# A fixed order for the first attention of a fused attention and two-MLP kernel, and other units kept on chip

## The chip, the cores and the metric
One core of a Trainium2 chip runs the kernel, in one launch. The metric is the device time of that launch in microseconds (us). The kernel before took 708.74 us (median of three runs, 707.78 to 709.10).

## The reference
Three layers follow each other, all in fp32:

```
attention, B=2, H=8, S=576, D=64:
  scores = q k^T / sqrt(D) + min(-(cum_i - cum_j), 0), causal   # cum: running sum of max(s, 0)
  attn   = softmax(scores);  x = attn v                         # 1152 tokens x 512
layer 1:  h = x w_in (512 x 2048);  g = h if h > 0 else exp(h) - 1;  x = g w_out
layer 2, four experts e, p = domain_probs normalised:
  out += p[:, e] * (max(x w1[e], 0) w2[e])                      # 512 x 1024 each
```

`moe_w_in` and `moe_w_out` come as 64-bit words; a part of the kernel turns them into fp32 ("decodes" them).

## The kernel before, in words
**Groups.** The 1152 tokens are worked on in three groups, of 256, 448 and 448 (`GROUPS`). Group 0 goes through attention, layer 1 and layer 2; then layer 1 runs for groups 1 and 2, and layer 2 for both together. The attention of group 1 is cut into some seventy parts that a `Background` object strews between the products of layers 1 and 2 of group 0; that of group 2 is strewn into layer 1 of group 1.

**Layer 1.** `w_in` and `w_out` are cut into 16 units (`NAB`) of 128 hidden columns. `layer1` (line 701) runs slots k = 0 to 17: slot k issues up-projection k (`up1`, line 729, called u0, u1, ...), then its activation (exp on line 733, relu on line 736, the combination `gt` on line 737), and down-projection k - 2 (`down1`, line 716), which adds into four banks `acc0` to `acc3`. A bank `up` is free again when line 737 has read it, and there are two.

**Decoding.** For group 0 a unit comes as two halves of 512 KB, 32 in the order (0,0), (1,0), (0,1), (2,0), ... `fetch_halves` (line 126) issues their loads on SP's queue into places borrowed from tiles that are not yet in use (`places`: `gt`, `wu`, `wr`, `cd`, `yh`, ...); the first 25 have a place of their own, the last 7 wait until an earlier half in the same place has been decoded. `decode_halves` (line 139) turns one half into fp32: on ScalarE (ACT) an Abs (line 158) and a copy to `z` (line 165; for the first four halves on VectorE, line 161), on VectorE (DVE) two words (lines 166 and 168). The ACT instructions are pinned behind everything traced before on ACT. A unit that is not kept on chip is also written to DRAM (`w_dec`, line 171, on POOL's queue) for the later groups; units 12 to 15 stay in `wr`. `DEC` says after which step of the first attention how many halves are decoded; `advance` (line 637) decodes on, two or three per slot, ahead of layer 1, and orders the loads (`fetch`) and splits (`prepare`, line 102: a copy on ACT and `split_lo`, line 87, on DVE) of the weights that follow.

**The first attention** (`attention_first`, line 265) does group 0: 256 tokens, eight heads in four pairs hp. Per pair: `scores` (products of q and k and of the bias parts `cump` and `cumm`, lines 313 to 323, a bank per head; heads 6 and 7 use the banks of heads 2 and 3 again), `probabilities` (DVE line 333, then an exponential on ACT, line 335), `normalise` (DVE), `transposes` (PE line 352, copied out by ACT on line 353) and `values` (PE line 361, copied by ACT on line 363). `cum_parts` writes the running sum and its parts to DRAM for the later groups, `cum_columns` (line 223) turns a piece of it into columns, `probabilities_of` (line 251) normalises the layer-2 weights. `keep_warm` (line 365) issues products of the identity that nobody reads.

**What sets the order.** A planner orders each engine's instructions, by program order and by when its own model takes them to be ready; `issue_after` queues a block behind an instruction on the same engine, and `keep_in_program_order` pins one. Tiles of a pool that closes give their bytes to the next one: a tile there waits for the users of the earlier tiles on its bytes. The pool `first` holds the tiles of the first attention and the places `cd`; when slot 14 begins its background part (`First`, line 762), it closes and the pool `att` takes its bytes, for the attention of groups 1 and 2. The first loads of that attention (lines 429 and 430 into `pt`) are queued behind the last coded half on SP.

Of the kernel before, what the change touches and what calls it, by code (L numbers as in the profile page):

```python
# [45 lines left out]
DEC = [1, 2, 3, 4]  # L46
# [4 lines left out]
N_WR, N_WU, N_GT, N_CD = 2, 1, 3, 5  # L51
# [3 lines left out]
def tile_kernel(ctx, tc, qT, kT, v, s, w64, w, probs, out):  # L55
# [39 lines left out]
    def fetch(n):  # L95
        if n >= NU and (n - NU) % NAB in kept:
            fetched[n] = kept[(n - NU) % NAB]
            return
        fetched[n] = t = sb([128, 1024], "raw", 3)
        SP.dma_start(out=t, in_=w[n - NAB] if n < NU else w_dec[(n - NU) % NAB])  # L100

    def prepare(n):
# [9 lines left out]
    small = [("yh", 1, 1), ("yl", 1, 1)] + [("raw", 3, 1)] * 3 + [("xa", 1, 3), ("ox", 1, 3)]  # L112
    turn = ([("gt", 3, 1)] * N_GT + [("wu", 5, 2)] * N_WU + [("wr", N_WR, 2)] * N_WR
            + [("cd", N_CD, 1)] * N_CD + small * 2)
# [9 lines left out]
    n_coded, n_decoded, last_coded = [0], [0], [None]  # L124
# [13 lines left out]

    def decode_halves(upto):

        while n_decoded[0] < min(upto, len(order)):
            i = n_decoded[0]
            n, part = order[i]
            if part == 0:
                if n % 2 == 0:
                    if n < NAB - N_KEPT:
                        pair = sb([128, 2, 1024], "wu", 5)  # L150
                    else:
                        pair = sb([128, 2, 1024], "wr", N_WR)
                        kept[n], kept[n + 1] = pair[:, 0], pair[:, 1]
                    units[n], units[n + 1] = pair[:, 0], pair[:, 1]
            x, m = coded.pop(i), units[n][:, 512 * part:512 * part + 512]
            high, low, mi = x[:, :, 1], x[:, :, 0], m.bitcast(I32)
            tc.keep_in_program_order(
                ACT.activation(m, high.bitcast(F32), AF.Abs, scale=2.0 ** -112))  # L158
            z = sb([128, 512], f"z{i % 2}", 1, I32)
            if i < N_LOW:  # L160
                tc.keep_in_program_order(DVE.tensor_scalar(
                    z, low.bitcast(U32), 7.49 / 2 ** 32, None, op0=ALU.mult))
            else:
                tc.keep_in_program_order(
                    ACT.activation(z, low.bitcast(U32), AF.Copy, scale=7.49 / 2 ** 32))  # L165
            DVE.scalar_tensor_tensor(out=mi, in0=mi, scalar=3, in1=z,
                                     op0=ALU.logical_shift_left, op1=ALU.bitwise_or)
            DVE.scalar_tensor_tensor(out=mi, in0=high, scalar=-2 ** 31, in1=mi,
                                     op0=ALU.bitwise_and, op1=ALU.bitwise_or)
            if part and n not in kept:  # L170
                POOL.dma_start(out=w_dec[n], in_=units[n])
            n_decoded[0] += 1
            fetch_halves()
# [3 lines left out]
    make_identity(nc, ident)  # L177

# [10 lines left out]

    zero = sb([64, 256], "zero", 1)  # L190
    POOL.memset(zero, 0.0)

# [69 lines left out]
    def attention_first(x):  # L265
# [31 lines left out]
        with tc.issue_after(high.ins), tc.issue_after(low.ins):  # L297
            cum_parts()
# [57 lines left out]
        def values(hp):  # L356
            o = ps(f"acc{(hp + 2) % 4}", 1)
            for c, q0 in ((0, 0), (1, 128)):
                for j in range(2):
                    h = 2 * hp + j  # L360
                    PE.matmul(o[64 * j:64 * j + 64, q0:n], vv[:, c, 64 * h:64 * h + 64],
                              ptt[:, h, 256 * c:256 + 128 * c], start=c == 0, stop=c == 1)
            ACT.activation(x[:, hp], o[:, :n], AF.Copy)
# [9 lines left out]
        with tc.issue_after(keep_warm(12).ins):  # L373
            first = scores(0)
            with tc.issue_after(first.ins), tc.issue_after(low.ins):
                cum_columns(0, 4)
                cum_columns(1, 4)
            scores(1)
            scores(2)
        probabilities(0)  # L380
        decode_halves(DEC[0])
        with tc.issue_after(scores(3).ins):
            keep_warm(6)
        probabilities(1)
        with tc.issue_after(normalise(0).ins):
            shares.extend((probabilities_of(0, n // 128), probabilities_of(T2, NCH)))
        with tc.issue_after(transposes(0).ins):
            keep_warm(4)
        probabilities(2)
        normalise(1)  # L390
        transposes(1)
        values(0)
        decode_halves(DEC[1])
        probabilities(3)
# [3 lines left out]
        decode_halves(DEC[2])  # L398
        normalise(3)
        transposes(3)  # L400
        values(2)
        values(3)
        decode_halves(DEC[3])
# [354 lines left out]
    attention_first(x_first)  # L758
    pr_first, pr_later = shares
    xs = [None, None, None]  # L760

    class First:
# [3 lines left out]
        def __call__(self, at):  # L766
            if at > BG_FROM[0]:
                if self.got is None:
                    first_stack.close()
# [13 lines left out]
    for c in range(NCC):  # L783
        ACT.activation(yh[:, c], yacc[c], AF.Copy)
        split_lo(yl[:, c], yacc[c], yh[:, c])
    pr = pr_first
# [316 lines left out]
```

## Time and profile before

| | us |
|---|---|
| median of three runs (lowest, highest) | 708.74 (707.78, 709.10) |
| the profiled execution, its own time | 710.54 |
| its span, first to last instruction | 708.4 |
| PE busy in the span | 696.6 (98%) |
| DVE busy | 561.7 (79%) |
| ACT busy | 382.4 (54%) |
| POOL busy | 15.6 (2%) |

All later numbers in us are counted from the start of the span. Timelines merge equal instructions that follow each other; their lengths overlap a little, so the spacing of two starts says more than a length. "Idle before" is the time that the engine stood still ahead of a row, with what it waited for. The clock of a window is the share of TensorE's full speed that the chip granted.

### The profile page before, as it was taken

To read this page: it belongs to the slowest core of one execution; us is meant where nothing else is said; L and a number is where in the kernel's file an instruction comes from. 1 tells how busy PE (TensorE), PEld (TensorE's weight loads), DVE (VectorE), ACT (ScalarE), POOL (GpSimd) and SP (SyncE) were. 2 spreads that over 40 slices of the span, in tenths; PEclk is the share of its full clock that TensorE was granted. 3 is DMA by queue.
4 is the path that set the end of the run, shared out by engine and by line. 5 is a ranking of instruction groups with operands and counts; after the bars stand their busy time and mean duration, and the time that the engine had idled before them with its cause. 6 is when DMAs were issued, how large, how long until landed. Compare 5 with 4: busy or idle time off the path is not lost.

```text
span 708.4 us, 10218 instructions
## 1 busy us (share of the span) xinstructions
PE 696.6 (98%) x3670; PEld 595.6 (84%) x3670; DVE 561.7 (79%) x1146; ACT 382.4 (54%) x773; POOL 15.6 (2%) x36
## 2 busy tenths in 40 slices
PE   8999999999999999999999999999999999999997
PEld 7888788887878887888899988888888888888886
DVE  7799788797868898876975469988888888788765
ACT  5799798786768788866644344322222223332320
POOL 5011000000000000000000000000000000000000
PEclk9899999999999999999999999999999999999999
DMA  8999855655554433113530000111111111111002
GB/s 299 409 368 373 271 174 154 193 166 157 174 185 140 141 125 102 41 47 128 210 140 0 1 1 0 60 60 60 60 61 59 60 60 59 61 60 59 1 0 105
DMA packets 34578, 85.45 MB, mean 121 GB/s; under 512 B 3440, under 2 KB 13888, under 8 KB 34528
## 3 DMA queue, kind: packets, MB, share of 16 engines
q1 hardware_dynamic: 32576, 78.23, 32.7%
q0 software_dynamic: 1952, 6.57, 2.3%
q8 instruction: 29, 0.48, 0.3%
q14 instruction: 21, 0.17, 0.1%
HBM read 75.88 MB, written 8.91 MB: 120 GB/s over the span
## 4 chain that ended last, share of the span: by engine, by line
PE 86%; ACT 7%; DVE 3%; issue 1%; DMA 1%; POOL 0%; SPq 0%; DVEq 0%; ACTq 0%; POOLq 0%
PE acc L626 38%; PE up L626 16%; PE att L938 11%; PE up L938 8%; PE att L581 3%; PE att L554 3%; ACT z L165 2%; ACT wu L158 2%; PE att L509 1%; PE att L502 1%; PE att L504 1%; DMA pt<-in_kT 1%; ACT e L736 1%; PE att L370 1%; PE acc L716 1%
## 5 line engine op out<-in xcount | busy, mean ns | idle before, releaser
L626 PE MATMUL acc<-w,h 128*128 128x512 f32 x672 | 172.0, 392 | 0.0
L626 PEld LDWEIGHTS acc<-w,h 128*128 128x128 f32 x672 | 126.1, 188 | 23.0 <-ACT h L948 0.2
L626 PE MATMUL acc<-gt,wu 128*128 128x448 f32 x384 | 87.8, 372 | 0.0
L948 ACT ACTIVATE h<-c 128x448 fp32r<-128x448 f32 x48 | 27.4, 573 | 111.7 <-DVE c L954 111.7
L683 DVE SCALAR_TENSOR_TENSOR ox<-acc,pr,ox 128x512 f32<-128x512 f32 x105 | 78.6, 748 | 11.1 <-PE acc L626 9.1
L87 DVE TENSOR_TENSOR wu<-raw,wu 128x1024 fp32r<-128x1024 f32 x56 | 68.4, 1223 | 19.5 <-ACT wu L106 17.3
L626 PEld LDWEIGHTS acc<-gt,wu 128*128 128x128 f32 x384 | 70.1, 188 | 7.8 <-issue 2.6
L106 ACT ACTIVATE wu<-raw 128x1024 fp32r<-128x1024 f32 x56 | 59.1, 1055 | 15.8 <-PE acc L626 14.1
L938 PE MATMUL att<-S,top 128*128 128x448 f32 x288 | 66.3, 365 | 0.0
L938 PEld LDWEIGHTS att<-S,top 128*128 128x128 f32 x288 | 54.0, 188 | 6.7 <-issue 0.2
L626 PE MATMUL acc<-wu,gt 128*128 128x512 f32 x192 | 56.8, 411 | 0.0
L626 PE MATMUL up<-yh,wu 128*128 128x256 f32 x256 | 52.5, 287 | 0.0
L949 DVE SCALAR_TENSOR_TENSOR h<-c,h 128x448 fp32r<-128x448 f32 x48 | 29.8, 623 | 18.7 <-ACT h L948 18.7
L938 PE MATMUL up<-x2a,top 128*128 128x448 f32 x192 | 44.2, 366 | 0.0
L626 PEld LDWEIGHTS up<-yh,wu 128*128 128x128 f32 x256 | 41.8, 190 | 2.6 <-issue 1.7
L626 PE MATMUL up<-xa,wu 128*128 128x448 f32 x192 | 43.5, 371 | 0.0
L626 PE MATMUL up<-ox,wu 128*128 128x448 f32 x192 | 41.5, 366 | 0.8 <-DVE e L741 0.8
L544 ACT ACTIVATE p<-p,nm 128x384 f32<-128x384 f32 (+4 forms) x56 | 34.5, 616 | 13.6 <-DVE nm L539 13.2
L948 ACT ACTIVATE h<-up 128x448 fp32r<-128x448 f32 x16 | 8.7, 545 | 59.5 <-PE up L938 59.5
L938 PEld LDWEIGHTS up<-x2a,top 128*128 128x128 f32 x192 | 35.9, 188 | 4.8 <-ACT p L963 0.6
L626 PEld LDWEIGHTS up<-ox,wu 128*128 128x128 f32 x192 | 36.0, 188 | 4.0 <-DVE e L741 1.1
L626 PEld LDWEIGHTS acc<-wu,gt 128*128 128x128 f32 x192 | 32.8, 189 | 6.9 <-issue 2.5
(215 smaller groups left out, 1245.6 us busy)
## 6 DMA issues: line engine op xcount, KB each, us to landing
raw<-in_w SPq DMA_DIRECT2D x38, 512.0 KB
raw<-in_w SPq DMA_DIRECT2D x16, 1024.0 KB
raw<-w_dec SPq DMA_DIRECT2D x24, 512.0 KB
w_dec<-wu POOLq DMA_DIRECT2D x12, 512.0 KB, 7.4
cd<-in_w SPq DMA_DIRECT2D x5, 512.0 KB
xa<-in_w SPq DMA_DIRECT2D x5, 512.0 KB
k<-in_kT SPq DMA_DIRECT2D x8, 288.0 KB
cbp<-cum_d SPq DMA_DIRECT2D x16, 144.0 KB
```

Of the source, the lines that this page charges most:

```text
L87: DVE.tensor_tensor(out=lo, in0=x, in1=hi.bitcast(F32), op=ALU.subtract)
L106: ACT.activation(t[:, 0], x, AF.Copy)
L158: ACT.activation(m, high.bitcast(F32), AF.Abs, scale=2.0 ** -112))
L165: ACT.activation(z, low.bitcast(U32), AF.Copy, scale=7.49 / 2 ** 32))
L544: ACT.activation(p, p, AF.Exp, bias=nm, scale=-1.0, accum_out=sm)
L554: PE.transpose(pt[:cb[c + 1] - cb[c], m, :], p[:, cb[c]:cb[c + 1]], ident)
L581: PE.matmul(o[64 * j:64 * j + 64, qs:nq], job["v"][:n, c, 64 * j:64 * j + 64], job["pt"][:n, j, c, qs:nq], start=c == 0, stop=c == n_c - 1)
L626: PE.matmul(o, a[m], b[n], start=first and i == 0, stop=last and i == 2)
L683: DVE.scalar_tensor_tensor(out=o_sb, in0=o, scalar=pr[:, i, e:e + 1], in1=o_sb, op0=ALU.mult, op1=ALU.add)
L938: PE.matmul(bank, tops[q][:, m, op, cs], x[:, n, c], start=first and c + i == 0, stop=c == 1 and i == 2, skip_group_check=True)
L948: ACT.activation(h[:, 0, u, cs], c, AF.Relu)
L949: DVE.scalar_tensor_tensor(out=h[:, 1, u, cs], in0=c, scalar=0.0, in1=h[:, 0, u, cs].bitcast(F32), op0=ALU.max, op1=ALU.subtract)
```

## The change
`attention_first` is traced in a region in which PE, ACT and DVE issue their instructions exactly as written. In it the order is new: scores 0 and 1, probabilities 0 and 1, scores 2 and 3, and then normalise, probabilities, transposes and values, staggered. The two later `keep_warm` blocks are gone and the first has 8 products for 12. The Abs of a half can be traced ahead of the rest of its decoding (`begin_half`). `cum_columns` and `probabilities_of` move to slot 14 of layer 1, on DVE behind the last decoded word. Units 0 to 3 are kept in `wr`, units 4 to 15 are written to DRAM. Coded halves use three `wu` tiles in place of one and two `wr`, and the last seven go into `cd`, `yh` and `yl` again, in place of `yh`, `yl`, `raw`, `xa`. `zero` is set before `mask`.

```diff
--- before.py
+++ after.py
@@ -43,12 +43,12 @@
 BG_FROM = [14, 0, 0]
 BG_TO = [1, 1, 0]
 
-DEC = [1, 2, 3, 4]
+DEC = [1, 2, 4]
 AHEAD = 10
 
 N_LOW = 4
 
-N_WR, N_WU, N_GT, N_CD = 2, 1, 3, 5
+N_WR, N_WU, N_GT, N_CD = 2, 3, 3, 5
 N_KEPT = 2 * N_WR
 
 @with_exitstack
@@ -97,7 +97,7 @@
             fetched[n] = kept[(n - NU) % NAB]
             return
         fetched[n] = t = sb([128, 1024], "raw", 3)
-        SP.dma_start(out=t, in_=w[n - NAB] if n < NU else w_dec[(n - NU) % NAB])
+        SP.dma_start(out=t, in_=w[n - NAB] if n < NU else w_dec[(n - NU) % NAB - N_KEPT])
 
     def prepare(n):
 
@@ -109,9 +109,9 @@
 
     order = [(0, 0)] + [h for n in range(NAB - 1) for h in ((n + 1, 0), (n, 1))] + [(NAB - 1, 1)]
 
-    small = [("yh", 1, 1), ("yl", 1, 1)] + [("raw", 3, 1)] * 3 + [("xa", 1, 3), ("ox", 1, 3)]
-    turn = ([("gt", 3, 1)] * N_GT + [("wu", 5, 2)] * N_WU + [("wr", N_WR, 2)] * N_WR
-            + [("cd", N_CD, 1)] * N_CD + small * 2)
+    twice = [("cd", N_CD, 1)] * N_CD + [("yh", 1, 1), ("yl", 1, 1)]
+    turn = ([("gt", 3, 1)] * N_GT + [("wu", 5, 2)] * N_WU + twice
+            + [("raw", 3, 1)] * 3 + [("xa", 1, 3), ("ox", 1, 3)] + twice + [("xa", 1, 3)])
     places = [(tag, bufs, n, i) for tag, bufs, n in turn for i in range(n)]
     coded, freed_by, last_in = {}, [], {}
     for i, (tag, bufs, many, k) in enumerate(places):
@@ -121,7 +121,7 @@
         else:
             freed_by.append(-1)
         last_in[tag][-1] = i
-    n_coded, n_decoded, last_coded = [0], [0], [None]
+    n_coded, n_decoded, last_coded, last_word = [0], [0], [None], [None]
 
     def fetch_halves(upto=len(order)):
 
@@ -136,6 +136,21 @@
                                          in_=w64[n, :, 1024 * part:1024 * part + 1024])
             n_coded[0] += 1
 
+    begun = {}
+
+    def begin_half(i):
+        n, part = order[i]
+        if part == 0 and n % 2 == 0:
+            if n >= N_KEPT:
+                pair = sb([128, 2, 1024], "wu", 5)
+            else:
+                pair = sb([128, 2, 1024], "wr", N_WR)
+                kept[n], kept[n + 1] = pair[:, 0], pair[:, 1]
+            units[n], units[n + 1] = pair[:, 0], pair[:, 1]
+        begun[i] = m = units[n][:, 512 * part:512 * part + 512]
+        tc.keep_in_program_order(
+            ACT.activation(m, coded[i][:, :, 1].bitcast(F32), AF.Abs, scale=2.0 ** -112))
+
     def decode_halves(upto):
 
 
@@ -144,18 +159,10 @@
         while n_decoded[0] < min(upto, len(order)):
             i = n_decoded[0]
             n, part = order[i]
-            if part == 0:
-                if n % 2 == 0:
-                    if n < NAB - N_KEPT:
-                        pair = sb([128, 2, 1024], "wu", 5)
-                    else:
-                        pair = sb([128, 2, 1024], "wr", N_WR)
-                        kept[n], kept[n + 1] = pair[:, 0], pair[:, 1]
-                    units[n], units[n + 1] = pair[:, 0], pair[:, 1]
-            x, m = coded.pop(i), units[n][:, 512 * part:512 * part + 512]
+            if i not in begun:
+                begin_half(i)
+            x, m = coded.pop(i), begun.pop(i)
             high, low, mi = x[:, :, 1], x[:, :, 0], m.bitcast(I32)
-            tc.keep_in_program_order(
-                ACT.activation(m, high.bitcast(F32), AF.Abs, scale=2.0 ** -112))
             z = sb([128, 512], f"z{i % 2}", 1, I32)
             if i < N_LOW:
                 tc.keep_in_program_order(DVE.tensor_scalar(
@@ -165,16 +172,19 @@
                     ACT.activation(z, low.bitcast(U32), AF.Copy, scale=7.49 / 2 ** 32))
             DVE.scalar_tensor_tensor(out=mi, in0=mi, scalar=3, in1=z,
                                      op0=ALU.logical_shift_left, op1=ALU.bitwise_or)
-            DVE.scalar_tensor_tensor(out=mi, in0=high, scalar=-2 ** 31, in1=mi,
-                                     op0=ALU.bitwise_and, op1=ALU.bitwise_or)
+            last_word[0] = DVE.scalar_tensor_tensor(out=mi, in0=high, scalar=-2 ** 31, in1=mi,
+                                                    op0=ALU.bitwise_and, op1=ALU.bitwise_or)
             if part and n not in kept:
-                POOL.dma_start(out=w_dec[n], in_=units[n])
+                POOL.dma_start(out=w_dec[n - N_KEPT], in_=units[n])
             n_decoded[0] += 1
             fetch_halves()
 
 
     ident = sb([128, 128], "ident", 1)
     make_identity(nc, ident)
+
+    zero = sb([64, 256], "zero", 1)
+    POOL.memset(zero, 0.0)
 
     mask = sb([128, S], "mask", 1)
     POOL.memset(mask, 0.0)
@@ -186,13 +196,6 @@
         m = maskp[64 * j:64 * j + 64]
         POOL.affine_select(out=m, in_=m, compare_op=ALU.is_ge, fill=-BIG, base=0,
                            pattern=[[-1, 64]], channel_multiplier=1)
-
-    zero = sb([64, 256], "zero", 1)
-    POOL.memset(zero, 0.0)
-
-
-
-
 
 
     cum = sb([B * H, S], "cum", 1)
@@ -294,8 +297,7 @@
             high = ACT.activation(t[:B * H], cum[:, 0:n], AF.Copy, scale=sign)
             low = DVE.scalar_tensor_tensor(out=t[64:], in0=cum[:, 0:n], scalar=sign,
                                      in1=t[:B * H].bitcast(F32), op0=ALU.mult, op1=ALU.subtract)
-        with tc.issue_after(high.ins), tc.issue_after(low.ins):
-            cum_parts()
+        cum_parts()
 
 
 
@@ -354,7 +356,7 @@
             return last
 
         def values(hp):
-            o = ps(f"acc{(hp + 2) % 4}", 1)
+            o = ps(f"acc{hp}", 1)
             for c, q0 in ((0, 0), (1, 128)):
                 for j in range(2):
                     h = 2 * hp + j
@@ -370,37 +372,32 @@
                 last = PE.matmul(o, ident, ident, start=True, stop=True)
             return last
 
-        with tc.issue_after(keep_warm(12).ins):
-            first = scores(0)
-            with tc.issue_after(first.ins), tc.issue_after(low.ins):
-                cum_columns(0, 4)
-                cum_columns(1, 4)
-            scores(1)
-            scores(2)
-        probabilities(0)
-        decode_halves(DEC[0])
-        with tc.issue_after(scores(3).ins):
-            keep_warm(6)
-        probabilities(1)
-        with tc.issue_after(normalise(0).ins):
-            shares.extend((probabilities_of(0, n // 128), probabilities_of(T2, NCH)))
-        with tc.issue_after(transposes(0).ins):
-            keep_warm(4)
+        keep_warm(8)
+        for hp in (0, 1):
+            scores(hp)
+        for hp in (0, 1):
+            probabilities(hp)
+        for hp in (2, 3):
+            scores(hp)
+        normalise(0)
         probabilities(2)
+        transposes(0)
         normalise(1)
+        probabilities(3)
         transposes(1)
+        begin_half(0)
         values(0)
-        decode_halves(DEC[1])
-        probabilities(3)
         normalise(2)
         transposes(2)
         values(1)
-        decode_halves(DEC[2])
+        begin_half(1)
         normalise(3)
+        decode_halves(DEC[0])
         transposes(3)
         values(2)
+        decode_halves(DEC[1])
         values(3)
-        decode_halves(DEC[3])
+        decode_halves(DEC[2])
 
 
     def attention_parts(g, x):
@@ -755,8 +752,9 @@
 
 
     x_first = sb([128, NCC, GROUPS[0][1]], "xf", 1)
-    attention_first(x_first)
-    pr_first, pr_later = shares
+    with tc.manual_schedule(engines={mybir.EngineType.PE, mybir.EngineType.Activation,
+                                     mybir.EngineType.DVE}):
+        attention_first(x_first)
     xs = [None, None, None]
 
     class First:
@@ -766,6 +764,10 @@
         def __call__(self, at):
             if at > BG_FROM[0]:
                 if self.got is None:
+                    with tc.issue_after(last_word[0].ins):
+                        cum_columns(0, 4)
+                        cum_columns(1, 4)
+                        shares.extend((probabilities_of(0, n_tile), probabilities_of(T2, NCH)))
                     first_stack.close()
                     att_pool[0] = att_stack.enter_context(
                         tc.tile_pool(name="att", bufs=1, reuse_waits="tile"))
@@ -783,6 +785,7 @@
     for c in range(NCC):
         ACT.activation(yh[:, c], yacc[c], AF.Copy)
         split_lo(yl[:, c], yacc[c], yh[:, c])
+    pr_first, pr_later = shares
     pr = pr_first
     oacc = {}
     osb = sb([128, n_tile, DM], "xf", 1)
```

## Rows read from the trace of the kernel before

**Rows 1.** Page, part 1: engine busy us (share of span) x instructions.
```profile
PE 696.6 (98%) x3670; PEld 595.6 (84%) x3670; DVE 561.7 (79%) x1146; ACT 382.4 (54%) x773; POOL 15.6 (2%) x36
```

**Rows 2.** Waits of PE after 90 us: total us, times, longest (first and last).
```profile
PE up L626 <- DVE e L741: 0.8, 1, 0.8
...
PE att L554 <- DVE sm L517: 0.2, 1, 0.2
```

**Rows 3.** Windows: busy us of each engine, PE clock, DMA share, GB/s.
```profile
10.00:15.00 5.00, 3.77 (x29) 2.66 (x28) 4.62 (x22) 3.24 (x11) 0.00 (x0) 1.00 1.03 386
15.00:20.00 5.00, 5.00 (x25) 5.00 (x26) 4.93 (x35) 2.88 (x12) 0.00 (x0) 0.50 1.03 406
20.00:25.00 5.00, 5.00 (x37) 3.86 (x37) 2.45 (x11) 3.91 (x11) 0.00 (x0) 0.81 1.02 412
40.00:50.00 10.00, 10.00 (x48) 8.79 (x48) 9.55 (x18) 9.90 (x21) 1.60 (x3) 1.00 0.99 393
60.00:80.00 20.00, 18.68 (x86) 15.57 (x85) 17.44 (x29) 17.67 (x33) 0.78 (x2) 1.00 1.01 351
```

**Rows 4.** Timeline of PE: start, length, instruction, count, [idle before <- releaser].
```profile
13.98 0.92 PE L313 MATMUL acc<-pt 64*128 64x128 f32 x6 [1.24 <-DVE nm L333]
...
16.56 2.77 PE L370 MATMUL att<-ident 128*128 128x128 f32 x12
...
20.54 1.77 PE L370 MATMUL att<-ident 128*128 128x128 f32 x8
...
22.90 0.87 PE L361 MATMUL acc<-pt 128*64 128x256 f32 x8
...
28.34 5.01 PE L729 MATMUL up<-xf,wu 128*128 128x256 f32 x22
...
39.51 1.99 PE L729 MATMUL up<-xf,wu 128*128 128x256 f32 x8 [0.83 <-DVE gt L737]
...
79.53 0.33 PE L502 MATMUL att<-kh,qs 128*128 128x128 f32 x1 [1.21 <-ACT kh L491]
```

**Rows 5.** Timeline of ACT.
```profile
8.32 0.40 ACT L335 ACTIVATE k<-k,nm 128x128 f32<-128x128 f32 x1 [1.56 <-DVE nm L333]
...
8.72 0.49 ACT L335 ACTIVATE k<-k,nm 128x256 f32<-128x256 f32 x1
...
24.66 0.85 ACT L353 ACTIVATE pt<-att 128x384 f32<-128x384 f32 x2
25.42 0.39 ACT L363 ACTIVATE xf<-acc 128x256 f32<-128x256 f32 x1
25.70 0.68 ACT L158 ACTIVATE wu<-gt 128x512 f32<-128x512 f32 x1
26.28 0.86 ACT L353 ACTIVATE pt<-att 128x384 f32<-128x384 f32 x2
...
29.94 0.38 ACT L733 ACTIVATE e<-up 128x256 f32<-128x256 f32 x1 [0.54 <-PE up L729]
...
69.82 0.71 ACT L165 ACTIVATE z<-xa 128x512 int32<-128x512 uint32 x1
```

**Rows 6.** Timeline of DVE.
```profile
6.09 0.55 DVE L228 COPY cum<-cum 16x64 f32<-16x64 f32 x3
6.57 1.40 DVE L219 SCALAR_TENSOR_TENSOR rows<-cum,rows 16x576 fp32r<-16x576 f32 x2
...
72.38 1.22 DVE L87 TENSOR_TENSOR wu<-raw,wu 128x1024 fp32r<-128x1024 f32 x1 [0.67 <-ACT wu L106]
73.52 0.69 DVE L168 SCALAR_TENSOR_TENSOR wr<-xa,wr 128x512 int32<-128x512 int32 x1
```

**Rows 7.** Timeline of SP's queue.
```profile
66.50 3.34 SPq L100 DMA_DIRECT2D raw<-in_w  x3
```

**Rows 8.** Chain that ended last, 66 to 81 us: start, length, what.
```profile
70.44 6.92 DMA pt<-in_kT
```

**Rows 9.** Page, part 6: DMA issues, count, KB each, us to landing.
```profile
w_dec<-wu POOLq DMA_DIRECT2D x12, 512.0 KB, 7.4
```

## The prediction

> **What bounds the kernel now.** I read the page first. TensorE (PE) is busy for 98% of the span [rows 1], so only stretches in which it stands still, or does work that the result does not need, can give time back. The waits of PE after 90 us show where little is left: four lines, from 0.8 us down to 0.2 us [rows 2]. So the run from 90 us on is as long as PE's work, and the change can act only on the first 90 us; whatever it gains there stays gained. The windows of that stretch show two things [rows 3]. From 60 to 80 us PE is busy 18.68 of 20 us, ACT 17.67 and the DMA engines all the time. From 15 to 25 us PE is "busy" without a gap, but its granted clock is 0.50 and then 0.81: at half (1.2 GHz instead of 2.4) from 15.0 to about 21.9 (0.81 of 5 us is 1.9 us at half). PE's own timeline says what it does there [rows 4]. It waits 1.24 us before 13.98, runs 12 keep-warm products (2.77 us), transposes, 8 more keep-warm products (1.77 us), transposes and values; the first block of up-projections that runs without a break starts only at 28.34. ACT's timeline [rows 5] gives the anchors. The first exponential is at 8.32, the first exp of layer 1 (line 733, call it e0) at 29.94, and the last `z` of the decoding ends at 69.82 + 0.71 = 70.53: between e0 and there, 40.6 us, no row of ACT notes idle time. PE stops once more in this layer, 1.21 us before 79.53, where the first score product of the background attention waits for q and k.
>
> So there are two clocks to follow: when e0 comes, and, hung on e0 by the 40.6 us, when decoding ends and the background attention can load.
>
> **The change, part by part.** The sum is made against the profiled execution, 710.54 us of which the span is 708.4; that is 1.8 above the median of the runs, 708.74. I carry differences over to the median.
>
> *Opening.* VectorE (DVE) loses the column copies of `cum_columns`: three in 0.55 us at 6.09 and a fourth after the `rows` pair, which starts at 6.57 and takes 1.40 [rows 6]. The `rows` pair stays in front of the first scores, now fixed there, and its second half cannot start before ACT has made its input (about 6.8), so it ends near 7.5 and the first exponential moves from 8.32 to about 7.85: -0.45. Fewer keep-warm products at the start (8 for 12) cost nothing: the scores wait either way for `cumm`, which DVE makes just before the copies at 6.09.
>
> *From the first exponential to e0.* Now 29.94 - 8.32 = 21.6 us. In the new order PE has all scores behind it by about 13 (score group 4 no longer meets the 1.24 us wait, as `probabilities(0)` and `(1)` are done first), and ACT is the long chain. Its work: 16 exponentials, a short and a long one start 0.40 and 0.49 after each other, eight pairs, 7.1 us; 8 copies of transposes, 0.38 each, 3.0; 4 copies of values, 0.28, 1.1; 2 Abs of `begin_half`, 0.58, 1.2: 12.4 us (start to start, from 24.66 to 26.28 in rows 5). Waits I count at 1.4: about 0.5 at probabilities(2) and the first transposes, 0.9 before the last copy, since values(3) (eight products, 0.87 with their tail [rows 4]) must follow the last transposes' copy. Then 0.1 of hand-over, one up-projection (22 products in 5.01 us [rows 4], so eight in 1.8) and 0.2 of pipeline: 7.85 + 12.4 + 1.4 + 2.1 = 23.8 for e0. That is 6.1 earlier than 29.94, the opening's 0.45 included. The two keep-warm blocks (4.5 us) and the decode words of halves 0 and 1 between the normalisations are what goes. Ends: -7.5 without any of these waits; -4.7 with 0.7 more at two hand-overs.
>
> *What the keep-warm products did.* They are gone and the new order has its own holes: about 1.0 us of PE idle near 16 (transposes(2) wait for ACT's copies) and 0.5 twice near 20.5. In the trace a hole of 1.24 us was followed by half clock 1.0 us later, for 6.9 us [rows 3, 4]. I take it that this happens again. At half clock values(2) and values(3), which stand in the chain at its end, take about 0.8 more each [rows 4]: +1.6. Ends: 0 if the clock holds, +5.0 if u0 and u1, the first two up-projections, are also at half (2 x 1.7 more).
> The Trainium skill (TensorE: Matmul & The Clock Gate, Part 4: PE-mode transpose) says that transposes do not count as PE work for the clock as products do; by that rule taking the products out from between the transposes costs more than I count, and no row here separates the two. It is the third rival.
>
> *Decoding.* Same work per half, so 40.6 us from e0 to the last `z`: 64.4 instead of 70.5 before the clock's 1.6. The coded halves of the second round now go into the five `cd` buffers, free after half 9 decodes instead of 14, so they are ordered earlier; SP no longer blocks on `raw`, whose three loads wait for decoding until 66.50 today [rows 7]. I cost this at nothing, as ACT never waits for a coded half in rows 5; the cover is a lead of a few us. The four writes to DRAM of units 0 to 3 go and those of units 12 to 15 come: twelve either way, 7.4 us to land [rows 9].
>
> *The wait that is added.* `cum_columns` is now put on DVE behind the last decoded word, and it reads `cum`. The pool `att` takes the place of the pool `first`, and its first tile, `pt` (6 KB in a partition), lies on the first tiles there, `zero` (1 KB) and `cum` (2.3 KB). So its loads (SP, lines 429 and 430), and behind them in SP's queue everything else of that attention, will wait for those copies. From the last `z`: two words of DVE at 0.69 and a hand-over, 1.4 (the last one starts at 73.52 now, held back by a `split_lo` of 1.22 at 72.38 [rows 6]); four copies, 0.7; SP's issue of q before k, 0.45. k is issued at e0 + 43.2. It lands 6.92 us later in the trace (70.44 to 77.36), and the product follows 2.15 after that [rows 4, 8]. The third `raw` load, 512 KB ahead of it in the same queue, is gone: at 351 GB/s (60 to 80 us, [rows 3]) 1.5 us less, so 5.4. The product is then ready at e0 + 50.7; now it comes at e0 + 49.6 (79.53 - 29.94). Extra +1.1. Ends: -1.2, if k lands in 3.1 us and the product is ready when PE comes (today's wait goes as well), and +5.1: 1.5 more if the last DRAM writes take the `raw` load's place, and 2.5 if two `split_lo` stand before the last word on DVE.
>
> *The rest at nothing.* Other bank names for values; `probabilities_of` (eight short DVE operations) behind the decoding, where DVE has room; its two small loads behind the DRAM writes on POOL's queue, wanted only at the first eviction. In the two later passes units 0 to 3 instead of 12 to 15 need no load; rows 2 are the cover (PE never waits for a load there). Without it each late 512 KB load would cost 1.5 us.
>
> Sum: -6.1 + 1.6 + 1.1 = -3.4 us, so 708.7 - 3.4 = **705.3 us**.
>
> **Rivals.**
> *The clock holds and the wait vanishes.* For it: the clock did not fall after the 0.83 us hole before 39.51 [rows 3, 4]; PE could do u15 while it waits. -6.1 - 1.2 = -7.3: 701.4; with only one of the two, 703 to 704.
> *The DMA engines are the bound.* They run at 0.99 to 1.03 of their time in all windows of rows 3. If coded halves come no faster, only the shortfall can be saved: 351 GB/s over the 20 us from 60 against the 412 of the window at 20 us leaves 3 us. -3.0 + 1.1: 706.8. Against it: two megabytes of writes move behind the reads.
> *The clock stays low into layer 1* (the rule above, as a mechanism here): +5.0 in place of +1.6, 708.7: the change gives back what it took.
> *Slower: the added wait takes over.* Place: the product that starts at 79.53 now. Price: two `split_lo` ahead of the last word and writes in the queue make the extra 5.1, so PE stands 6.3 us, and after a hole like that the clock falls as at 15.0, for 6.9 us on a stretch where PE is the bound: 3.4 more. -6.1 + 1.6 + 5.1 + 3.4 = +4.0: 712.7. It decides once clock and wait together pass 6.1 us.
>
> **How the numbers follow.** Forecast 0.47; clock and wait both kind, or one of them, 0.22; DMA bound 0.12; low clock into layer 1 0.08; added wait 0.11. What a measurement of this kernel can tell from no change is about 0.2%, 1.4 us, so faster means under 707.3. From the forecast 0.42, the kind case 0.22 and the DMA case 0.09 are faster: 0.73. Same: 0.05, 0.03, 0.06 of the low clock and 0.02 of the added wait: 0.16. Slower: 0.02 and 0.09: 0.11. The range runs from the best case to just beside the third rival: 701.5 to 708.4, and leaves out the slower case and a part of the first and third; the forecast's own ends are 703.5 and 707.
>
> **What would show it.** Right: the first exponential near 7.85, e0 at 24 to 26, no keep-warm between transposes, the last `z` 40 to 41 us after e0, `pt` loads on SP right after copies of `cum`, and PE's one long wait before line 502's product. The clock step is wrong if the granted clock never falls between 13 and 30 us. The forecast as a whole is wrong if e0 is later than 28, if ACT has idle time on a coded half, or if PE's waits after 90 us grow.

## The result: slower, 715.3 us for 708.9, and the profile after

The changed kernel takes 715.29 us (median of 5 runs, 714.60 to 716.48), the kernel before 708.9 beside it (5 runs); the ratio is 1.0091, 95% interval 1.0078 to 1.0104. That is 6.4 us slower, where 3.4 us faster was forecast, and outside the range. Line numbers below are those of the changed kernel unless said otherwise; an experiment's can differ from them by up to four, and those of e4 and e10 go by the kernel before.

The page and the windows of the stretches shown before (columns as in [rows 3]) place it:

```profile
PE 695.3 (98%) x3642; PEld 590.7 (83%) x3642; DVE 561.5 (79%) x1146; ACT 381.6 (54%) x773; POOL 15.5 (2%) x36
```
```profile
10.00:15.00 5.00, 4.75 (x40) 3.81 (x40) 4.83 (x30) 4.80 (x20) 0.00 (x0) 1.00 1.03 384
15.00:20.00 5.00, 4.23 (x37) 2.80 (x38) 4.64 (x16) 5.00 (x17) 0.00 (x0) 1.00 1.03 407
20.00:25.00 5.00, 5.00 (x27) 3.64 (x27) 4.24 (x9) 3.96 (x10) 0.00 (x0) 1.00 1.03 419
60.00:80.00 20.00, 14.48 (x59) 11.86 (x58) 12.61 (x34) 11.21 (x21) 1.60 (x3) 0.83 0.65 243
```

PE's work is as long as it was [rows 1]. From 10 to 25 us the granted clock is 1.00 throughout, where it was 0.50 and 0.81 [rows 3]. From 60 to 80 us PE is busy 14.48 us instead of 18.68, at a mean clock of 0.83, and the DMA engines, full until then, are used at 0.65. After 90 us PE's waits are no longer than they were [rows 2]; these two are all:

```profile
PE up L623 <- DVE e L738: 0.8, 1, 0.8
PE att L551 <- DVE p L516: 0.6, 2, 0.4
```

ACT's timeline and then PE's (answering to [rows 5] and [rows 4]) show the front gaining and then losing:

```profile
7.79 0.40 ACT L337 ACTIVATE k<-k,nm 128x128 f32<-128x128 f32 x1 [1.12 <-DVE nm L335]
...
22.81 0.38 ACT L730 ACTIVATE e<-up 128x256 f32<-128x256 f32 x1
...
56.10 0.66 ACT L172 ACTIVATE z<-cd 128x512 int32<-128x512 uint32 x1
63.71 1.06 ACT L106 ACTIVATE wu<-raw 128x1024 fp32r<-128x1024 f32 x1 [6.95 <-DMA raw<-in_w]
...
70.01 0.68 ACT L172 ACTIVATE z<-yl 128x512 int32<-128x512 uint32 x1
```
```profile
16.52 0.93 PE L354 MATMUL att<-ident,k 128*128 128x128 f32 x6 [0.77 <-DVE sm L342]
...
56.87 1.89 PE L726 MATMUL up<-xf,wu 128*128 128x256 f32 x8
...
66.00 3.78 PE L726 MATMUL up<-xf,wu 128*128 128x256 f32 x8 [5.52 <-DVE gt L734]
...
71.48 1.89 PE L726 MATMUL up<-xf,wu 128*128 128x256 f32 x8
...
83.71 0.33 PE L499 MATMUL att<-kh,qs 128*128 128x128 f32 x1 [1.72 <-ACT kh L488]
...
88.46 1.99 PE L713 MATMUL acc<-gt,wu 128*128 128x256 f32 x8 [1.70 <-DVE gt L734]
```

In the kernel before, PE started units 11 and 13 here:

```profile
63.97 1.89 PE L729 MATMUL up<-xf,wu 128*128 128x256 f32 x8
...
70.87 1.89 PE L729 MATMUL up<-xf,wr 128*128 128x256 f32 x8
```

The first exponential of layer 1 comes at 22.81 instead of 29.94, and PE starts unit 11 at 56.87 instead of 63.97, so 7.1 us are in hand. Then ACT stands 6.95 us at line 106, the Copy of `prepare` for unit 16, until its `raw` load lands. The work that stands behind it in ACT's queue is the exponential of unit 11 and the Abs and `z` of the last four coded halves; in e1 below the same work runs on without a stand, so it was ready. PE runs dry, stands 5.52 us, and does the next unit at half clock (3.78 us for what takes 1.89). Unit 13 (the third row of line 726) starts at 71.48; before it was 70.87. The 7.1 us are gone, and 0.6 with them.

The second loss comes with the next attention. The chain of waits, SP's waits and its queue (answering to [rows 8] and [rows 7]):

```profile
45.72 17.89 DMA raw<-in_w
...
72.96 0.48 DVE cum L231 x4
...
74.63 1.14 DVE wu L87
75.83 0.33 SPq L100
76.33 4.99 DMA pt<-in_qT
```
```profile
SPq L100 <- DVE wu L87: 22.9, 2, 22.1
```
```profile
45.72 30.44 SPq L100 DMA_DIRECT2D raw<-in_w  x5
76.33 0.41 SPq L426 DMA_DIRECT2D pt<-in_qT  x1
```

The `raw` load is issued at 45.72 instead of 66.50 and lands 17.89 us later. Two more fetches (units 19 and 20) stand ahead of the `pt` loads in SP's queue; they wait 22.9 us in all for the splits of units 16 and 17 (line 87, on DVE behind the copies of `cum`) to free their buffers. So `pt` goes out at 76.33, 2.9 us after the copies of `cum` that I had taken for the last thing in front of it, and the first product of line 499 comes at 83.71 (before: 79.53), after 1.72 us of PE idle time; 1.70 more follow before 88.46.

### The profile page after: what moved, and what is told of

Its sections match the earlier page's. It is cut to its first block, busy times and chain, and to the rows that moved or that the text cites. A ratio compares the mean times of both kernels' runs of the same rounds, so it can differ in the third digit from the quotient of the medians.

```text
span 713.0 us, 10153 instructions
## 1 busy us (share of the span) xinstructions
PE 695.3 (98%) x3642; PEld 590.7 (83%) x3642; DVE 561.5 (79%) x1146; ACT 381.6 (54%) x773; POOL 15.5 (2%) x36
## 4 chain that ended last, share of the span: by engine, by line
PE 85%; ACT 6%; DVE 4%; DMA 3%; issue 1%; POOL 0%; SPq 0%; DVEq 0%; ACTq 0%; POOLq 0%
PE acc L623 38%; PE up L623 16%; PE att L941 11%; PE up L941 8%; PE att L578 4%; PE att L551 3%; DMA raw<-in_w 3%; ACT z L172 2%; PE att L506 1%; ACT wu L152 1%; PE att L499 1%; DVE wu L87 1%; PE att L501 1%; DMA pt<-in_qT 1%; PE att L372 1%
```

## The experiments

First theory: ACT's queue order. The split of unit 16 was put ahead of the last four halves because its load can now be issued early. Rivals: the added wait (late columns); DMA engines too full for any order; the new attention itself. Each ratio is to the kernel before, run beside the experiment on the same chip; 0.0014 of a ratio is 1 us. The kernel after stands at 1.0091.

| run | what | median us | ratio to before [95%] |
|---|---|---|---|
| e1 | split of unit 16 late | 710.69 | 1.0034 [1.0016, 1.0053] |
| e2 | columns and shares early | 708.31 | 0.9991 [0.9982, 0.9999] |
| e3 | attention only, late columns | 714.98 | 1.0088 [1.0075, 1.0101] |
| e4 | placing only | 711.91 | 1.0046 [1.0033, 1.0060] |
| e5 | columns at a fixed early place | 709.70 | 1.0007 [0.9992, 1.0021] |
| e6 | e1 and e5 | 706.52 | 0.9968 [0.9954, 0.9982] |
| e7 | e3 with e5's columns | 707.99 | 0.9992 [0.9977, 1.0006] |
| e8 | no writes of decoded units (part of the output is other numbers) | 708.70 | 1.0010 [0.9987, 1.0033] |
| e9 | e6 and `bias` late | 704.86 | 0.9950 [0.9934, 0.9966] |
| e10 | e9's order, old attention | 707.61 | 0.9989 [0.9980, 0.9998] |
| e11 | e8 again, one execution, for its trace | 710.69 | |

**e1_prepare_late.**
```diff
+                last_z[0] = ACT.activation(z, low.bitcast(U32), AF.Copy, scale=7.49 / 2 ** 32)
...
-            prepare(prepare_at[0])
+            with tc.issue_after(last_z[0].ins), tc.issue_after(last_word[0].ins):
+                prepare(prepare_at[0])
```


> The kernel after, with the split of units 16 and up (lines 106 and 87) queued on ACT and DVE behind the last decoded half; loads, places and everything else as they are. Theory (ACT's queue order: the 6.95 us that ACT stands at line 106 for `raw`, with four halves and an exponential behind it, is what pushes the run back): ACT runs on, the idle row of 5.52 us before PE's u12 (66.00) goes, the granted clock stays at 1.00 between 62 and 70, the last `z` ends near 63 to 65 instead of 70.69, and the time falls by 6 to 9 us, to about 706.5 to 709. Rival (DMA-bound: the DMA engines are full from 30 to 60 us and the last coded halves land no sooner than the `raw`): the wait only moves from line 106 to line 152, the last `z` stays near 68 to 70, 713 to 715. Rival (the late columns: the added wait and the `pt` loads behind it set the loss): the stall goes but the products of line 499 still stand, and the time falls by at most 2 us, to 713 or more.

Nothing is taken away but the place in the queues, and 4 us come back (1.0091 to 1.0034). The stall is gone and the last `z` ends at 63.77, so the coded halves were there: the DMA rival falls. But 710.7 is above the 706.5 to 709 expected. ACT's rows, then PE's, show a second wait:

```profile
63.10 0.67 ACT L171 ACTIVATE z<-yl 128x512 int32<-128x512 uint32 x1
63.67 1.05 ACT L106 ACTIVATE wu<-raw 128x1024 fp32r<-128x1024 f32 x1
...
75.43 0.63 ACT L483 ACTIVATE qs<-pt 64x512 fp32r<-64x512 f32 x1 [4.45 <-DMA pt<-in_qT]
```
```profile
77.81 0.33 PE L499 MATMUL att<-kh,qs 128*128 128x128 f32 x1 [2.53 <-ACT kh L488]
...
82.56 3.59 PE L714 MATMUL acc<-gt,wu 128*128 128x256 f32 x8 [0.66 <-DVE gt L735]
```

ACT waits 4.45 us for `pt`, PE 2.53 at line 499, and later products run at half clock (3.59 us for eight).

**e2_columns_early.**
```diff
+    cum_columns(0, 4)
+    cum_columns(1, 4)
+    shares.extend((probabilities_of(0, GROUPS[0][1] // 128), probabilities_of(T2, NCH)))
     xs = [None, None, None]
```


> The kernel after, with cum_columns and probabilities_of called right behind the first attention again, without the wait for the last decoded word; in SP's queue the three `pt` loads then stand ahead of the fourth and fifth fetch of line 100. The split of unit 16 keeps its place ahead of the last four halves. Theory (ACT's queue order): the 6.95 us stall and the clock fall stay; only the 1.72 us that PE stands at line 499 goes, 712 to 714. Rival (the late columns): most of the loss goes, and with the shorter attention the time is below before's, 703 to 706. Rival (DMA-bound): as after or some tenths less, 714 to 715.5.

Much faster than my theory allowed, though above the 703 to 706 of the late columns alone, and not a clean test: DVE waited for the `pr` load ahead of the attention, the first exponential came at 13.10, and so ACT reached line 106 only at 63.67, when `raw` had landed. Two waits went at once; e5 separates them.

**e3_attention_only and e4_placing_only.** In e3 the tags, `N_WU` and the kept units are as before; in e4 these alone are as after.


> The kernel after with only the placing put back: the last four units kept, `wu` for one turn, the `small` tags twice, so `raw` takes coded halves a second time and its first load for unit 16 can't be issued before those are decoded. The new order of the attention and the late columns stay. Theory (ACT's queue order, which the early `raw` load brings): no split ahead of a decode, no ACT stall, the attention's gain of about 7 us at the first exponential of layer 1 (22.8) is kept up to the last `z`, near 63 to 65; six fetches stand ahead of the `pt` loads on SP, which costs 1 to 3 us of it at line 499: 703.5 to 706.5. Rival (DMA-bound): the decoding can't end before about 68, whatever the order, and the gain is at most 2 us: 706.5 to 709. Rival (the late columns, or the fixed order of the attention, is what costs): 711 to 715.

> The kernel before with only the placing changed as in the kernel after: first four units kept, three `wu` places for coded halves, `raw` given to coded halves once. Attention, its order and the columns are before's. Theory (ACT's queue order): the split of unit 16 stands ahead of the last four halves here too, but ACT comes to it some 7 us later (near 63.5) while the load lands near 64 to 66, so it stands 1 to 3 us: 709 to 712. Rival (DMA-bound): the demand is the same and ACT is later, so nothing waits, 708 to 709.5. Rival (the fixed order of the attention costs the loss): 708.7, no change, and no stall.

My first theory fails on both. In e3 no split stands ahead of a decode, and the loss is as large as after's, where the third account (late columns or fixed order) had put it. ACT, then PE:

```profile
56.25 0.68 ACT L152 ACTIVATE wr<-yh 128x512 f32<-128x512 f32 x1 [0.73 <-DMA yh<-in_w]
...
60.15 0.68 ACT L152 ACTIVATE wr<-raw 128x512 f32<-128x512 f32 x1 [0.62 <-DMA raw<-in_w]
```
```profile
56.08 3.68 PE L726 MATMUL up<-xf,wu 128*128 128x256 f32 x8 [2.67 <-DVE gt L734]
...
83.20 0.33 PE L499 MATMUL att<-kh,qs 128*128 128x128 f32 x1 [2.65 <-ACT kh L488]
...
85.90 3.78 PE L713 MATMUL acc<-gt,wr 128*128 128x256 f32 x8 [0.42 <-DVE gt L734]
```

With the old places ACT, being 7 us early, catches up with the coded halves (six waits, 4.6 us in all); then PE stands 2.65 us at line 499, with the columns late and six fetches ahead of `pt`, and runs at half clock behind it. e4's time is within what was expected, for another reason: ACT came to line 106 at 63.05 without idle time. PE (lines as in the kernel before) stands later, in the next attention, with a clock of 0.85 from 80 to 90 and 0.81 from 90 to 100. Why it stands there I did not isolate; e10, which differs from e4 only in the split and `bias` coming late, is 4.0 us faster:

```profile
85.21 0.30 PE L504 MATMUL att<-kl,qb 68*128 68x128 f32 x1 [1.22 <-DMA kl<-rows_d]
...
87.58 0.47 PE L502 MATMUL att<-kh,qs 128*128 128x128 f32 x1 [1.46 <-DVE nm L539]
```

**e5_columns_fixed and e6_both.**
```diff
         decode_halves(DEC[2])
+        cum_columns(0, 4)
+        cum_columns(1, 4)
```
(In slot 14 the two lines go.)


> The kernel after with cum_columns alone moved: in the fixed order it now stands right behind the last decode of the first attention, while probabilities_of stays behind the last decoded word (in e2_columns_early its `pr` load held the first exponential to 13.10, so that ACT came to line 106 late). Order of the split of unit 16 as in after. Theory (two waits in series, ACT's 6.95 us at line 106 and, behind it, the `pt` loads held on SP by the late columns and two fetches): the stall and the half clock from 62 to 70 stay, the three `pt` loads go ahead of the fourth fetch, and the stand at line 499 (1.72 us) and at line 713 (1.70 us) go: 711 to 713. Rival (the late columns alone make the loss, as e2_columns_early's 708.3 could say): 702 to 706. Rival (ACT's stall alone, and e2_columns_early gained by its late start only): 714 to 715.5.

> e1_prepare_late and e5_columns_fixed together: split of unit 16 behind the last decode, columns at a fixed place early. Theory (two waits in series): PE's u12 near 61.3 as in e1_prepare_late, no stand of over 1 us at lines 499 and 713, full clock between 75 and 90, the first layer ends some 6 to 7 us before the 87.0 of the kernel before, and the time is 701.5 to 704. Rival (DMA-bound: with the front 7 us earlier the loads of the next attention arrive late in their turn): 706 to 708.5. Rival (a third wait behind both): 708.5 to 711.

New theory: two waits in series. With e1, e5 and e6 all four combinations are there: as it is 1.0091, split late 1.0034, columns early 1.0007, both 0.9968. The first edit is worth 4.0 us alone and 2.8 on top of the second, the second 6.0 and 4.7. Neither alone beats the kernel before; both together do. In e5 the `pt` loads go out at 51.43, ahead of the fetches of units 19 and 20, and the stall on ACT stays. SP first, then ACT and PE:

```profile
51.43 0.38 SPq L428 DMA_DIRECT2D pt<-in_qT  x1
```
```profile
62.68 1.06 ACT L106 ACTIVATE wu<-raw 128x1024 fp32r<-128x1024 f32 x1 [4.66 <-DMA raw<-in_w]
```
```profile
64.96 3.51 PE L728 MATMUL up<-xf,wu 128*128 128x256 f32 x8 [3.11 <-DVE gt L736]
```

Moving the columns puts `pt` ahead of the two fetches at the same time; what the copies and what the fetches cost by themselves, no run separates. The time is 1.3 us under the expected 711 to 713. The profiled execution, 2.0 us below the median, would fit that: its `raw` load landed a microsecond earlier, and ACT came 1.3 us later (first exponential of layer 1 at 23.51, for 22.81). e6 is above the 701.5 to 704 expected, within 706 to 708.5, where the loads of the next attention arrive late in their turn. DVE, then PE:

```profile
75.72 0.49 DVE L250 TENSOR_SCALAR bias<-cbp,cum_p 128x512 f32<-128x512 f32 x1 [2.10 <-DMA cbp<-cum_d]
...
77.45 0.75 DVE L737 SCALAR_TENSOR_TENSOR gt<-up,e 128x256 f32<-128x256 f32 x2
```
```profile
77.92 4.54 PE L716 MATMUL acc<-gt,wu 128*128 128x256 f32 x12 [1.94 <-DVE gt L737]
```

DVE stands 2.10 us for `cbp`, the `gt` of the last units behind it; PE stands 1.94 us and runs twelve products in 4.54 us.

**e7_attention_columns.** 

> e3_attention_only with the columns at the fixed early place: the new order of the attention with before's placing, columns early. Theory (in e3_attention_only the coded halves landed late for ACT, PE stood 2.67 us at 56.08 and ran the next unit at half clock, 1.8 us more; then 2.65 us at line 499): the first part stays, the second goes, the first layer ends near 83 instead of 87.0: 704 to 706.5. Rival (with before's placing the loads can't follow and all of the gain is lost): 708 to 710. Rival (placing costs nothing, the columns were all of it): 701 to 703.

707.99: against e3 the early columns give 6.8 us. Against e6 the old places cost 1.5 to 1.7, so the new placing may have a small value of its own once nothing stands behind its early load; the two intervals overlap. And e7 has of the change little more than the new attention, with the old places and the columns early: its first exponential of layer 1 comes at 23.70, 6.2 us earlier than before, and its time is that of the kernel before.

**e8_no_writes and e11_no_writes_look.**
```diff
-                POOL.dma_start(out=w_dec[n - N_KEPT], in_=units[n])
+                pass
```


> The kernel after without the twelve writes of decoded units; the later loads of those units read second-layer units instead, the same bytes. That part of the output is other numbers. Order of instructions as in after. Theory (the `raw` load takes 18 us from issue to landing because it queues behind some 6 MB of coded halves and writes on full DMA engines): some ten writes of 0.52 MB at 420 GB/s less, 12 us, `raw` lands near 52, before ACT comes to line 106 at 56.8; no stall there, the late columns stay: 709.5 to 711.5 as e1_prepare_late. Rival (the landing is late for another reason than the bytes in front of it): the stall at line 106 stays within 2 us of its 6.95, 713 to 715.

> The kernel of e8_no_writes again (the twelve writes of decoded units left out, later loads read second-layer units instead), for its trace: in the profiled execution of e8_no_writes the first loads came late and all behind them some 7 us. Theory (`raw` queues behind the bytes in front of it): it lands by 52 to 55 instead of 63.71, no idle time of over 0.5 us before line 106, DMA engines near idle between 58 and 70, PE's u12 at full clock; the stand at line 499 stays at 1.5 to 3 us. Rival: `raw` lands after 60 and ACT stands at line 106.

708.70, 5.7 us under the kernel after by the ratios, at the far end of what was expected (4 to 6). In e11 (an execution 2.0 us above e8's median) ACT's row and the windows from 60 on:

```profile
56.60 1.09 ACT L106 ACTIVATE wu<-raw 128x1024 fp32r<-128x1024 f32 x1
```
```profile
60.00:72.00 12.00, 12.00 (x58) 10.30 (x57) 11.17 (x31) 7.96 (x16) 0.00 (x0) 1.00 0.27 83
72.00:80.00 8.00, 4.85 (x19) 3.80 (x17) 2.71 (x7) 4.90 (x9) 0.00 (x0) 0.79 0.98 294
```
```profile
77.39 0.47 PE L499 MATMUL att<-kh,qs 128*128 128x128 f32 x1 [3.15 <-ACT kh L488]
```

With the same order of instructions and the writes (0.52 MB each) out of the way, `raw`, issued at 44.27, is there when ACT comes at 56.60, and the DMA engines run at 0.27 from 60 to 72. So at least 5.6 of the 17.89 us were queueing behind the writes (12.3 us at most are left). The added wait remains (PE's last row: 3.15 us).

**e9_bias_late and e10_old_attention.**
```diff
+                    with tc.issue_after(last_gt[0].ins) if g == 1 else nullcontext():
+                        add_bias(it["bias"], job["cump"][:, 0], cum_p[b][:, hp:hp + 1], d0, d1, maskp)
```


> e6_both with one thing more: the two DVE instructions of add_bias (lines 250 and 251) for the next attention queued behind the first layer's last `gt`. In e6_both DVE stood 2.10 us at line 250 for `cbp`, with the `gt` of the last two units behind it, and PE stood 1.94 us at 77.92 and ran twelve products at half clock (4.54 us for what takes 2.8 at full clock). Theory (one in-order queue after the other passes the wait on to PE, and the clock doubles it): both go, 3 to 3.5 us: 702.5 to 704.5. Rival (the next attention needs `bias` and its loads then, so the wait only moves behind 82 us): 705.5 to 707.

> The order of e9_bias_late (split of unit 16 behind the last decode, add_bias behind the last `gt`, columns early) and the new placing, but with the attention of the kernel before, its keep-warm products and the planner's order. It shows what the new attention is worth where no later queue gives its gain back. Theory: e9_bias_late's front is 6 us earlier (first exponential of layer 1 at 24 against 29.9) and keeps most of it: this one 3.5 to 6 us above e9_bias_late, 706.5 to 709. Rival (the DMA engines, full from 10 to 70 us, set the end of the first layer): within 2 us of e9_bias_late.

e9 is the fastest version here, 704.86 us, below both kernels (0.9950, 0.9934 to 0.9966). It gains 1.3 us on e6, not 3, and the two intervals overlap: PE's holes are now 0.44 and 0.54 us and the clock stays at 1.00.

```profile
72.80 0.33 PE L501 MATMUL att<-kh,qs 128*128 128x128 f32 x1 [0.44 <-ACT kh L490]
...
77.28 1.99 PE L717 MATMUL acc<-gt,wu 128*128 128x256 f32 x8 [0.54 <-DVE gt L738]
```

e10 is 2.8 us above e9 (0.9989 to 0.9950), between theory and rival. Its first exponential of layer 1 is at 29.24, e9's at 23.66: of 5.6 us in front, half reaches the end. PE's rows say where the other half goes; e9's start of unit 4 and of layer 2, then e10's:

```profile
34.10 1.99 PE L730 MATMUL up<-xf,wu 128*128 128x256 f32 x8
...
81.73 0.34 PE L626 MATMUL up<-yh,wu 128*128 128x256 f32 x1
```
```profile
38.82 1.99 PE L731 MATMUL up<-xf,wu 128*128 128x256 f32 x8 [0.86 <-DVE gt L739]
...
84.58 0.34 PE L627 MATMUL up<-yh,wu 128*128 128x256 f32 x1
```

At unit 4 e9 leads by 4.7 us, at layer 2 by 2.85. From 60 us to there PE stands 1.24 us in e9 and not at all in e10. The loads of the next attention go out no earlier with the new attention. In both, SP's issue of the third `pt` load takes over 7 us, and the next load follows at 63.77 in e9 and 62.65 in e10:

```profile
56.10 7.57 SPq L429 DMA_DIRECT2D pt<-in_v  x1
```
```profile
54.83 7.73 SPq L430 DMA_DIRECT2D pt<-in_v  x1
```

In e9 ACT then stands 3.23 us for `pt` before 69.85, with the DMA engines at 1.04 to 1.07 from 64 to 72. That the full DMA engines take the other half fits these rows; no run takes bytes away from e9 to show it.

## Why the prediction was wrong, step by step

*Opening and attention: right.* First exponential 7.79 (7.85 forecast); first exponential of layer 1 at 22.81, 1.0 better than the 23.8, and 7.1 us earlier than before where 6.1 was counted. That this gain stays ("whatever it gains there stays gained") was not right: by e9 and e10 half of it reaches the end, even with split, columns and `bias` all moved.

*Clock, +1.6: wrong.* It never fell between 13 and 30 us; the holes were 0.26, 0.77 and the like. The Trainium skill (TensorE: Matmul & The Clock Gate, Part 4: PE-mode transpose) says that transposes do not count as PE work for the clock in the same way; 24 of them between 12.95 and 19.06, with values products among them, went by at 1.00 here. By that rule as I had made it a rival the change would have lost up to 5 us; the trace does not bear that out for this mix. Nor does the fall belong to the old order as such: with the old attention the clock from 15 to 20 us was 0.50 in the kernel before, 0.66 in e4 and 1.00 in e10.

*Decoding, "I cost this at nothing": the step that failed.* I wrote that "SP no longer blocks on `raw`" and looked only at whether ACT waits for coded halves. It does not; it waits for `raw`. That load, free to go 21 us earlier, had the planner put the split that needs it ahead of the last four halves (so also in e4, and not in e3, where the load stays late), and the load went into DMA engines that stayed full (1.02 to 1.03 until 64 us). From the first exponential of layer 1 to the last `z` the trace has 7.3 us more than forecast; e1 prices the step at 4.0 us, or 2.8 on top of the early columns. The 40.6 us from the first exponential of layer 1 to the last `z` were right for the work itself: with the split behind them, e1 needs 39.95 (23.82 to 63.77) and e6 40.5; the kernel after needs 47.9.

*The added wait, +1.1 (ends -1.2 and +5.1): place right, size wrong.* From the last `z` to the issue of k I had 2.6 us; it was 6.1 (70.69 to 76.79), because two fetches that wait for splits stand before `pt` on SP. The landing of `pt` (4.99 for q, against 5.4 for k) was about right. From the last `z` to the first product of line 499 it is 13.0 us, where the kernel before has 9.0: 4.0 more in place of 1.1. By e6 over e1, where the first stall is gone from both, moving the columns is worth 4.7; the 6.0 of e5 holds a shorter first stall too (4.66 on ACT for 6.95).

*Rivals.* The slower rival (712.7, chance 0.11) came nearest. Its late product is here; its clock fall is here too, but behind the stall on ACT, which it left out. Behind the late product the clock stayed at 1.00 in the kernel after (80 to 90 us) and fell to 0.50 in e1 (80 to 85 us). DMA as the bound of the decoding is not the cause: in e1 the same bytes move and the last `z` is 6.9 us earlier than after's 70.69. It decides only what an early load costs to whoever waits for it (e8, e11), how far the old places can follow (e3) and, it may be, what is lost of the gain in e9.

*The rest at nothing: right to about a microsecond.* PE's waits after 90 us did not grow. The kernel after lies 3.5 us behind at the first `yh` (89.20 against 85.67) and 4.6 at the end of the profiled spans (708.4 and 713.0; the medians lie 6.4 apart, as the execution profiled before was about 1.8 above its median); where the last 1.1 us goes no run shows. So the two traces add up: -7.1 in front, +7.3 in the decoding, +4.0 from the last `z` to the product, -0.7 from there to `yh`, +1.1 behind it.

So the sum failed by leaving out one wait and by undersizing another. It also counted the whole front as gained: with these two waits mended e6 is 2.3 us below the kernel before, with `bias` late as well e9 3.5, where 6.1 was counted. That e9's 704.86 lies next to the forecast's 705.3 is chance: e9 has neither the clock's 1.6 nor the added wait's 1.1, and keeps only a part of the gain.

## What to carry to other kernels

When a front is shortened, list for every in-order queue (SP's too) which instruction waits for a load and what is queued behind it; a load that may start earlier can move its consumer ahead of ready work. Price the wait by the bytes in front of the load on full DMA engines, and allow for PE's half clock behind a long stand (here 5.52 us, then 3.78 for a unit that takes 1.89). Of two mendings neither may bring the time below the old kernel's alone, and both together may. Even then, ask whether the loads behind the front come earlier too: here they did not, and half of the gain was lost.

## What the hardware showed that I had not expected

- A 512 KB load took 17.89 us from issue to landing behind coded halves and writes, while SP's issue itself took 0.33 us; without the writes at most 12.3 us (44.27 to 56.60, e11).
- SP's own issue of a load can take long: the third `pt` load took 7.46 to 7.93 us in e2, e5, e6, e9 and e10, which issue it between 54 and 57 us with the DMA engines full, and 0.50 to 0.99 us in the other runs, which issue it after 68 us.
- PE's stand and the clock do not follow one length: 1.24 us before 13.98 was followed by 0.50 in the kernel before [rows 3, 4], 1.94 us in e6 by a fall (0.57 from 78 to 82), but 1.72 and 1.70 us in the kernel after (83.71, 88.46) and 1.75 us in e10 (20.45) by none: the clock is 1.00 from 80 to 90 and from 10 to 30. After the 5.52 us stand the clock was at 0.50 until close to 70 us (0.51 from 64 to 70), with PE busy again from 66.
